# Sparse attention into a mixture of experts on one core: both groups of sparse scores in one stretch, the block list as one row

## The chip, the cores and the metric

The kernel runs on one core of a Trainium2 chip. The metric is the device time of one execution in microseconds (us). The engines are named as in the profile: PE is TensorE (its weight loads are listed apart, as PEld), DVE is VectorE, ACT is ScalarE, POOL is GpSimd, SP is SyncE, which here only issues DMAs. TensorE writes to PSUM, which has eight banks.

## The reference, cut to what matters

Attention over 4 batches x 8 heads x 768 positions x 64, in blocks of 32 (24 blocks). A block of queries sees its own block and the two neighbours, the first and the last block, and three sampled blocks; the first and last query blocks see everything. The result goes, token by token, through a top-1 mixture of eight experts.

```python
mask = np.abs(blk_i - blk_j) <= window                      # window = 1
mask = mask | (blk_i == 0) | (blk_j == 0) | (blk_i == n_blocks - 1) | (blk_j == n_blocks - 1)
for qb in range(n_blocks):
    for kb in sampled_blocks[qb]:                           # three of 24, drawn at random
        mask[qb * block:(qb + 1) * block, kb * block:(kb + 1) * block] = True
scores = np.where(mask, scores, -1000000000.0)              # scores = q @ k.T / 8
attn = softmax(scores); x = (attn @ v) as (3072 tokens, 512)
logits = x @ w_gate + modality_bias[modality_id]
e_idx = argmax(logits); gate_w = softmax(logits)[e_idx]
out = gate_w * (relu(x @ w1[e_idx]) @ w2[e_idx])            # 512 -> 1024 -> 512, 8 experts
```

## The kernel before, in words

**Work items.** Attention is cut into items. A dense item ("d", batch, pair of heads) computes the two query blocks that see everything; there are 16, eight for each half of the batches. A sparse item ("s", half, m, n, b) belongs to a pair m of inner query blocks (11 pairs), query block n of the pair and batch b of the half. Scores of one (half, m, n) are computed for both batches and all heads at once, into two PSUM banks, so a pair m has two groups of scores, n=0 and n=1. The text of the prediction calls one (half, m) a sparse item; there are 22, numbered 0 to 21.

**Stages.** Each item passes stages named by letters: S scores (`dense_scores` L372, `scores` L525, TensorE), M mask and minimum or maximum (`masked` L537 with the operation at L541, VectorE), X exp (`exps` L546, ScalarE), T transposes (L558, L411, TensorE), A copy of the transposes out of PSUM (L563, L418), W weighing of the values (L580, L433), V the row sums and the sampled blocks' values (L573, L589), O division (L440 to L442), Y and G transpose and gate (L596, L606). The banks of scores are free when M of both batches has read them.

**Order.** The kernel writes the order of every engine's program out by hand (`tc.manual_schedule`). The start follows the list START of tokens: an upper case token such as `S00` is a stage of an item, `tb` is one step of the generator `tables()`, `SP16` sixteen such steps, `kl` a load of queries, `qp` the gathering of keys (`share_k` L462), `vl`, `vs` and `v` the gathering of values, `h` a tick's other work, `blk` the reading of the block list (L212). After that a loop over ticks runs stages in the order `OXTSMGVAYW`; in tick t each stage handles the item t minus that stage's lag (S 0, M 1, X 2, T 4, A 4, W 5, V 7, O 8, Y 10, G 13). A sparse pair takes four ticks; scores for n=0 come in the first of them and for n=1 in the third. PSUM banks come from a pool of eight; a matmul into a bank waits until its last readers are done.

**Gathered keys.** `share_k` on GpSimd copies the key blocks that a pair needs into one of two buffers of twelve slots: slots 0 to 7 for n=0, 4 to 11 for n=1. The sampled blocks are copied by number (L482, twelve copies a pair): the first six go to slots 0 to 2, the last six to slots 9 to 11. GpSimd reads the numbers into registers in `key_numbers` (L457), SyncE in `own_numbers` (L511).

**The start.** SyncE issues, in order: the block list broadcast to 128 partitions (L166, 72 KB), queries and keys of the dense items (`dense_q` L150, `dense_k` L157), values (L163), then the gate's inputs (L178 to L180), then by tokens `kl0` and `kl1` the first sparse queries (L144). TensorE runs 56 warm-up matmuls (L210) of 128x128. GpSimd takes the block numbers out of the list (L213), VectorE turns them to floating point (L243) and builds the mask tables (L247 to L274) and the modality bias (L278 to L288) step by step, sixteen steps before the first dense maximum (L392).

## Time and profile before

| | us |
|---|---|
| median of 3 runs (lowest to highest) | 539.94 (538.39 to 546.9) |
| the profiled execution | 535.39 |
| its span, from first to last instruction | 533.7 |
| PE busy, DVE busy, ACT busy, POOL busy in it | 512.8, 378.7, 335.4, 214.7 |

A row of the timeline gives start, duration, engine, source line, operation, what is written from what, and how many instructions were merged into it; in square brackets the engine's idle time before it and what ended that. "issue" means that it waited for nothing the profile shows. SPq rows are DMA issues, whose durations are the issue and not the transfer. A row of the table of stretches gives the stretch, its length, then busy time and number of instructions of each engine, the granted TensorE clock, the share of the DMA engines' time and GB/s; an instruction that runs over a border is counted in both stretches. In a row of a group (page, part 5) the numbers after the bar are the busy time of the group and the mean ns of one.

### The profile page before, as it was taken

To read this page: it belongs to the slowest core of one execution; us is meant where nothing else is said; L and a number is where in the kernel's file an instruction comes from. 1 tells how busy PE (TensorE), PEld (TensorE's weight loads), DVE (VectorE), ACT (ScalarE), POOL (GpSimd) and SP (SyncE) were. 2 spreads that over 40 slices of the span, in tenths; PEclk is the share of its full clock that TensorE was granted. 3 is DMA by queue.
4 is the path that set the end of the run, shared out by engine and by line. 5 is a ranking of instruction groups with operands and counts; after the bars stand their busy time and mean duration, and the time that the engine had idled before them with its cause. 6 is when DMAs were issued, how large, how long until landed. Compare 5 with 4: busy or idle time off the path is not lost.

```text
span 533.7 us, 19015 instructions
## 1 busy us (share of the span) xinstructions
PE 512.8 (96%) x7298; PEld 433.4 (81%) x7298; DVE 378.7 (71%) x1139; ACT 335.4 (63%) x765; POOL 214.7 (40%) x451
## 2 busy tenths in 40 slices
PE   8999999998999999899999999999999999999995
PEld 6667676776778777788989898998989899898984
DVE  7995588677778999967996655556565555656553
ACT  3689877977888977935456454646545464554552
POOL 3578675666458886123155123030312303031213
PEclk9999999999999999999999999999999999999999
DMA  7985886999646888965788776676757667675740
GB/s 281 339 243 150 234 252 209 249 223 242 205 144 205 209 217 233 277 206 206 237 280 305 237 253 201 239 252 204 239 191 244 211 222 250 206 243 192 249 150 23
DMA packets 49443, 119.44 MB, mean 224 GB/s; under 512 B 7744, under 2 KB 8128, under 8 KB 49344
## 3 DMA queue, kind: packets, MB, share of 16 engines
q1 hardware_dynamic: 45248, 105.02, 64.6%
q0 software_dynamic: 4096, 13.12, 6.9%
q8 instruction: 59, 0.97, 0.8%
q14 instruction: 40, 0.33, 0.2%
HBM read 105.52 MB, written 12.86 MB: 222 GB/s over the span
## 4 chain that ended last, share of the span: by engine, by line
issue 41%; PE 32%; DVE 11%; DMA 7%; POOL 5%; SPq 3%; ACT 1%; POOLq 0%; DVEq 0%; ACTq 0%
PE bank L533 5%; PE bank L558 5%; DMA out<-slot,si 3%; PE bank L589 3%; DVE y L541 3%; POOL slot L736 3%; DMA slot<-v 3%; PE bank L580 2%; POOL out L790 2%; PE bank L606 2%; PE bank L754 1%; PE bank L770 1%; PE bank L771 1%; PE bank L769 1%; PE bank L755 1%
## 5 line engine op out<-in xcount | busy, mean ns | idle before, releaser
L725 DVE TENSOR_TENSOR slot<-slot 128x1024 fp32r<-128x1024 f32 x99 | 122.8, 1245 | 89.5 <-ACT slot L722 87.7
L722 ACT CAST slot<-slot 128x1024 fp32r<-128x1024 f32 x104 | 108.1, 1048 | 104.1 <-PE bank L755 50.1
L754 PE MATMUL bank<-slot 128*128 128x256 f32 x384 | 108.4, 282 | 0.0
L756 PE MATMUL bank<-slot 128*128 128x256 f32 x384 | 107.7, 281 | 0.0
L755 PE MATMUL bank<-slot 128*128 128x256 f32 x384 | 107.6, 280 | 0.0
L790 POOL DMA_INDIRECT out<-slot,si x20 | 25.4, 1270 | 178.6 <-ACT slot L786 175.6
L549 ACT ACTIVATE a<-y,mn 128x256 f32<-128x256 f32 x176 | 88.6, 511 | 10.3 <-DVE mn L541 10.2
L769 PE MATMUL bank<-slot 128*128 128x512 f32 x192 | 76.6, 399 | 0.0
L770 PE MATMUL bank<-slot 128*128 128x512 f32 x192 | 75.9, 395 | 0.0
L771 PE MATMUL bank<-slot 128*128 128x512 f32 x192 | 75.7, 394 | 0.0
L754 PEld LDWEIGHTS bank<-slot 128*128 128x128 f32 x384 | 72.2, 188 | 0.6
L755 PEld LDWEIGHTS bank<-slot 128*128 128x128 f32 x384 | 72.1, 188 | 0.4
L756 PEld LDWEIGHTS bank<-slot 128*128 128x128 f32 x384 | 72.2, 188 | 0.0
L541 DVE CUSTOM_DVE_ANT_1 y<-bank,smask 128x256 f32<-128x256 f32 x176 | 66.3, 417 | 0.4
L482 POOL COPY slot<-slot 128x128 f32 x264 | 63.9, 295 | 0.0
L563 ACT COPY at<-bank 128x512 f32<-128x512 f32 x88 | 50.7, 577 | 9.9 <-PE bank L558 9.9
L504 POOL TENSOR_SCALAR slot<-slot 32x1024 f32<-32x1024 f32 x40 | 41.6, 1041 | 35.4 <-issue 11.6
L558 PE MATMUL bank<-ident,a 128*128 128x128 f32 x352 | 51.9, 280 | 0.8 <-ACT a L401 0.5
L533 PE MATMUL bank<-slot,q_raw 64*32 64x256 f32 x1408 | 49.4, 382 | 1.5 <-issue 0.6
L771 PEld LDWEIGHTS bank<-slot 128*128 128x128 f32 x192 | 36.1, 188 | 8.4
L770 PEld LDWEIGHTS bank<-slot 128*128 128x128 f32 x192 | 36.1, 188 | 7.8 <-DVE slot L725 0.4
L558 PEld LDWEIGHTS bank<-ident,a 128*128 128x128 f32 x352 | 38.1, 140 | 4.9 <-ACT a L549 0.8
(302 smaller groups left out, 852.9 us busy)
## 6 DMA issues: line engine op xcount, KB each, us to landing
slot<-w SPq DMA_DIRECT2D x100, 512.0 KB, 4.1
slot<-v SPq DMA_DIRECT2D x180, 128.0 KB, 3.9
x_d<-xr SPq DMA_DIRECT2D x22, 256.5 KB, 5.0
q_raw<-qH SPq DMA_DIRECT2D x22, 256.0 KB, 4.8
slot<-v SPq DMA_DIRECT2D x16, 256.0 KB, 4.6
slot<-kD SPq DMA_DIRECT2D x13, 256.0 KB, 4.3
slot<-v SPq DMA_DIRECT2D x4, 768.0 KB, 11.8
slot<-w SPq DMA_DIRECT2D x10, 256.0 KB, 4.1
```

The costliest lines, as they stand in the source:

```text
L533: nc.tensor.matmul(sp[u][32 * pr:32 * pr + 32, b * 256:(b + 1) * 256], lhsT=q[r, b * NPAIR + pr, n, :], rhs=kv[r, s0:s0 + 8, b, pr, :], st ...
L541: nc.vector.tensor_tensor_reduce(y[:, u, :].rearrange("p (s f) -> p s f", s=8), sp[u][:, b * 256:(b + 1) * 256].rearrange("p (s f) -> p s ...
L549: nc.scalar.activation(a[:, u, :], y[:, u, :], AF.Exp, bias=mn[:, u:u + 1], scale=-1.0, accum_out=total[:, u:u + 1])
L558: nc.tensor.transpose(tp[:, k:k + P], a[:, u, c * P:(c + 1) * P], ident)
L722: nc.scalar.copy(h, s)
L725: (eng or (nc.gpsimd if n in POOL_SPLITS else nc.vector)).tensor_tensor(l, s, h.bitcast(F32), ALU.subtract)
L754: nc.tensor.matmul(o, lhsT=h[:, fs], rhs=xh[g % 2][:, c, :], start=c == 0 and f % 2 == 0, stop=False)
L755: nc.tensor.matmul(o, lhsT=h[:, fs], rhs=xl[g % 2][:, c, :], start=False, stop=False)
L756: nc.tensor.matmul(o, lhsT=l[:, fs], rhs=xh[g % 2][:, c, :], start=False, stop=c == 3 and f % 2 == 1)
L769: nc.tensor.matmul(o, lhsT=hh[0][:, f, ts_], rhs=h[:, fs], start=f == 0, stop=False)
L770: nc.tensor.matmul(o, lhsT=hh[0][:, f, ts_], rhs=l[:, fs], start=False, stop=False)
L771: nc.tensor.matmul(o, lhsT=hl[f // 4][:, f % 4, ts_], rhs=h[:, fs], start=False, stop=f == 7)
```

## The change

1. For every sparse pair but the very first, TensorE computes the scores of n=0 and n=1 directly after one another, at the place of n=0. M and all later stages stay where they were.
2. The block list is loaded as one row (1 partition, 576 bytes) on ScalarE's DMA queue. The numbers, cast to bf16 by VectorE, are spread to 128 partitions by a matmul with a row of ones, between the warm-up matmuls, which are now 14 before and 24 after it; VectorE copies the result out of PSUM.
3. The mask tables are built by GpSimd: ten steps where sixteen of VectorE's stood (the cast of the numbers is no step of the tables any more), and eleven between the two batches' key copies of the first pair. Five `tb` tokens remain, for the modality bias on VectorE.
4. SyncE issues the first piece of keys first, then queries, then the other keys. The gate's inputs are issued by a new token `sm` after `kl1`. GpSimd reads the first pair's key numbers right after the list.

```diff
-WARM = 56
+WARM = (14, 24)
 START = """
-blk SP16 S00 S01 M00 S02 M01 X00 T00 X01 M02 T01 M03 X02 A00 T02 X03 A01 T03 kl0 S10 S11 A02 tb tb M10 A03 tb tb X10 M11 qp0
-W00 X11 O00 W01 tb tb T10 O01 A10 W02 kl1 T11 S12 S13 O02 A11 M12 W03 X12 M13 S0000 S0001 h8 X13 O03 T12 M0000 A12 M0001 W10
+blk SP10 S00 S01 M00 S02 M01 X00 T00 X01 M02 T01 M03 X02 A00 T02 X03 A01 T03 kl0 S10 S11 A02 M10 A03 X10 M11 qp0
+W00 X11 O00 W01 T10 O01 A10 W02 kl1 sm T11 S12 S13 O02 A11 M12 W03 X12 M13 S0000 S0001 h8 X13 O03 T12 M0000 A12 M0001 W10
...
-        blk_raw = const.tile([P, NB * 3 * 2], I32, name="blk_raw")
-        nc.sync.dma_start(blk_raw, blocks.bitcast(I32).rearrange("a b -> (a b)").partition_broadcast(P))
-        dense_q(0, 0, 4)
+        blk_raw = const.tile([1, NB * 3 * 2], I32, name="blk_raw")
+        nc.scalar.dma_start(blk_raw, blocks.bitcast(I32).rearrange("a b -> (a b)").unsqueeze(0))
...
-        dense_k(0)
+        dense_k(0, (0,), ((0, 16),))
+        dense_q(0, 0, 4)
+        dense_k(0, (0,), ((16, 24),))
+        dense_k(0, (1,))
         dense_q(0, 4, 8)
         dense_k(1, (0,))
         dense_v(0)
         dense_k(1, (1,))
         dense_v(1)
-        nc.sync.dma_start(wg_raw, ...)
-        nc.sync.dma_start(mod_raw..., ...)
-        nc.sync.dma_start(b_raw..., ...)
+
+        def gate_inputs():
+            nc.sync.dma_start(wg_raw, ...)
+            nc.sync.dma_start(mod_raw..., ...)
+            nc.sync.dma_start(b_raw..., ...)
...
         warm = bank()
-        for _ in range(WARM):
-            nc.tensor.matmul(warm[:, 0:P], lhsT=onesb, rhs=onesb, start=True, stop=True)
+        ids = blk_raw.rearrange("p (n t) -> p n t", t=2)[:, :, 0:1].rearrange("p n t -> p (n t)")
+        spread_ids = bank()
+
+        def warm_up(n):
+            for _ in range(n):
+                nc.tensor.matmul(warm[:, 0:P], lhsT=onesb, rhs=onesb, start=True, stop=True)

         def block_ids():
-            nc.gpsimd.tensor_copy(rb_i, blk_raw...)
+            nc.gpsimd.tensor_copy(rb_i, ids)
+            key_numbers(0)
...
             nc.vector.tensor_copy(iota_f, iota_i)
+            nc.vector.tensor_copy(rb_b, ids)
+            warm_up(WARM[0])
+            nc.tensor.matmul(spread_ids[:, 0:NB * 3], lhsT=onesb[0:1, :], rhs=rb_b, start=True, stop=True)
+            warm_up(WARM[1])
+            nc.vector.tensor_copy(rb, spread_ids[:, 0:NB * 3].rearrange("p (n t) -> p n t", t=3))
             nc.vector.tensor_scalar(desc, iota_f[:, 0:E], -1.0, float(E), ALU.mult, ALU.add)
...
         def tables():
-            nc.vector.tensor_copy(rb, rb_i.rearrange("p (n t) -> p n t", t=3))
-            yield
-            nc.vector.tensor_tensor(t0, rb, iota_f[:, 0:NB].unsqueeze(2).broadcast_to([P, NB, 3]), ALU.subtract)
+            nc.gpsimd.tensor_tensor(t0, rb, iota_f[:, 0:NB].unsqueeze(2).broadcast_to([P, NB, 3]), ALU.subtract)
             yield
...
@@ share_k
             for bs in ((0,), (1,)) if g == 0 else (range(HB),):
+                if bs == (1,):
+                    spare(11)
                 if m < 2:
...
-        loads = {"blk": block_ids}
+        loads = {"blk": block_ids, "sm": gate_inputs}
...
                 if op == "S":
                     if b == 0:
-                        sp = scores(qraw[m, half], half * NM + m, n)
-                        for b_ in range(HB):
-                            st["s", half, m, n, b_] = sp
+                        for n_ in (n,) if (half, m) == (0, 0) else range(2) if n == 0 else ():
+                            sp = scores(qraw[m, half], half * NM + m, n_)
+                            for b_ in range(HB):
+                                st["s", half, m, n_, b_] = sp
```

All 21 operations of the mask tables (seven on 128x72 elements, twelve on 128x24, two on 128x33) go from `nc.vector` to `nc.gpsimd` in the same way as the one shown.

More of the change, by code (lines that the diff above doesn't have):

```diff
@@ L155, in dense_k @@
             for c in cs:
-                for j0, j1 in js or (((0, 16), (16, 24)) if (b, c) == (0, 0) else ((0, 24),)):
+                for j0, j1 in js or ((0, 24),):
                     nc.sync.dma_start(kd[b][:, c, j0:j1, :].rearrange("p j f -> p (j f)"), kD[b, :, c, j0 * 64:j1 * 64])
@@ L177, in attention_moe @@
         dense_v(1)
-        nc.sync.dma_start(wg_raw, w_gate.rearrange("(c p) e -> p c e", p=P))
-        nc.sync.dma_start(mod_raw.rearrange("p n t -> p (n t)"), modality.bitcast(I32))
-        nc.sync.dma_start(b_raw.rearrange("p a e -> p (a e)"), bias.rearrange("a e -> (a e)").partition_broadcast(P))
+        def gate_inputs():
+            nc.sync.dma_start(wg_raw, w_gate.rearrange("(c p) e -> p c e", p=P))
+            nc.sync.dma_start(mod_raw.rearrange("p n t -> p (n t)"), modality.bitcast(I32))
+            nc.sync.dma_start(b_raw.rearrange("p a e -> p (a e)"), bias.rearrange("a e -> (a e)").partition_broadcast(P))
         onesb = const.tile([P, P], BF16, name="onesb")
@@ L196, in attention_moe @@
         code = const.tile([P, NT], F32, name="code")
-        rb_i = const.tile([P, NB * 3], I32, name="rb_i")
+        rb_i = const.tile([1, NB * 3], I32, name="rb_i")
+        rb_b = const.tile([1, NB * 3], BF16, name="rb_b")
         rb = const.tile([P, NB, 3], F32, name="rb")
```

25 lines of the change are left out of this document (12 added, 13 removed).

## The prediction

> **What bounds the kernel now.** I read the page's busy times first, then the table of stretches, then TensorE's own timeline in one item of the sparse phase, then the first 24 us.
>
> ```profile
> PE 512.8 (96%) x7298; PEld 433.4 (81%) x7298; DVE 378.7 (71%) x1139; ACT 335.4 (63%) x765; POOL 214.7 (40%) x451
> ```
> ```profile
> core 0: us, PE busy (x) PEld busy (x) DVE busy (x) ACT busy (x) POOL busy (x), PEclk, DMA share, GB/s
> 10.00:20.00 10.00, 8.99 (x139) 6.40 (x132) 9.12 (x34) 8.27 (x29) 2.86 (x12) 1.00 1.04 382
> ...
> 30.00:40.00 10.00, 9.04 (x201) 6.80 (x186) 9.64 (x44) 8.14 (x28) 9.27 (x31) 1.00 0.84 242
> 100.00:120.00 20.00, 19.16 (x494) 14.83 (x502) 14.20 (x75) 16.25 (x53) 12.55 (x37) 1.00 0.92 224
> 200.00:220.00 20.00, 17.91 (x445) 13.60 (x441) 19.18 (x95) 17.28 (x52) 9.12 (x18) 1.00 0.90 245
> 300.00:400.00 100.00, 100.00 (x646) 90.45 (x645) 60.78 (x66) 52.08 (x64) 19.89 (x18) 1.00 0.68 224
> ```
>
> Three regimes. Up to 40 us VectorE is nearly full (9.1 to 9.6 us of 10) and TensorE follows it. In the body of the sparse phase TensorE is the fullest (19.16 of 20) and VectorE has room (14.20). Around 200 to 220 us VectorE is full again (19.18). From then on the experts keep TensorE at 100.00 of 100, so that whatever is saved before simply moves the end. The diff touches the first two regimes; no operation of the experts changes.
>
> **Scores in one stretch.** For 21 of the 22 sparse items the second group of scores (query block n=1) moves from two ticks later to right behind the first. No matmul is added or removed, so what can be saved is the cost of entering and leaving the stretch. TensorE's weight loads, and the matmuls of one stretch cut into windows:
>
> ```profile
> 149.97 0.20 PEld L431 LDWEIGHTS bank<-su,ident 128*64 128x64 f32 x4 [0.17 <-issue]
> 150.94 0.42 PEld L558 LDWEIGHTS bank<-ident,a 128*128 128x128 f32 x4
> 151.52 0.61 PEld L533 LDWEIGHTS bank<-slot,q_raw 64*32 64x32 f32 x32 [0.17 <-issue]
> 152.55 0.20 PEld L431 LDWEIGHTS bank<-su,ident 128*64 128x64 f32 x4 [0.41 <-DVE rd L447]
> ```
> ```profile
> 151.50:151.70 0.20, 0.17 (x8) 0.18 (x16) 1.00 0.37 144
> 151.70:151.92 0.22, 0.22 (x16) 0.16 (x9) 1.00 0.13 19
> 151.92:152.13 0.21, 0.21 (x24) 0.15 (x8) 1.00 0.00 0
> ```
>
> A stretch holds TensorE from 151.52 to 152.55, 1.03 us. It enters 0.17 after the transposes and the next work follows 0.41 after its last weight load. But the 0.41 is not all lost time: each window of 0.21 to 0.22 us brings eight more matmuls (the counts, 8, 16, 24, include those still running), so the 32 go in four rounds of about 0.215, and the 0.41 falls into the last round's running out. A second stretch appended to the first therefore costs four more rounds, 4 x 0.215 = 0.86, where it costs 1.03 alone. The entry of 0.17 is not saved either: what then follows the transposes at the old place is the 64- or 32-column work, and L431 at 149.97 enters after transposes with the same 0.17. That is 0.17 per item, 21 x 0.17 = 3.5 us off TensorE. Some two items lie in 200 to 220 us, where VectorE is full and the saving need not arrive: 3.2.
>
> The Trainium skill, TensorEngine Tiling (Array Packing), Key Properties, says that a change of the tiling mode drains TensorE. By that rule alone one would book entry and exit, 0.17 + 0.41 = 0.58 for each item, 12.2 us in all; it is rival A.
>
> **The banks that this takes.** The second group's two PSUM banks are now taken about 0.86 us after the first group's start, and held till VectorE reads them (L541) on ticks 3 and 4. TensorE then waits wherever fewer than two of the eight banks are free. An ordinary place, and the two tight ones:
>
> ```profile
> 103.56 1.09 PE L533 MATMUL bank<-slot,q_raw 64*32 64x256 f32 x32
> 104.08 0.42 DVE L541 CUSTOM_DVE_ANT_1 y<-bank,smask 128x256 f32<-128x256 f32 x1
> 104.13 0.62 ACT L563 COPY at<-bank 128x512 f32<-128x512 f32 x1
> ```
> ```profile
> 138.00 1.18 PE L533 MATMUL bank<-slot,q_raw 64*32 64x256 f32 x32
> 139.57 0.47 ACT L402 ACTIVATE a<-bank,nb__3730 128x256 f32<-128x256 f32 x1
> ```
> ```profile
> 209.03 1.09 PE L533 MATMUL bank<-slot,q_raw 64*32 64x256 f32 x32
> 210.25 0.15 DVE L440 TENSOR_SCALAR rt<-bank 128x8 f32<-128x8 f32 x1
> ```
>
> At 103.56 + 0.86 = 104.42 five banks are taken: two of the new scores, two of the item before (their last readers, L541, run 104.08 to about 104.8), one of a transpose (its copy L563 ends at 104.75). Three are free, no wait. At 138.86 seven are taken, four of them by dense scores, and the second free bank comes with the exp (L401) that ends where L402 begins, 139.57: 0.7. At 209.89 all eight are taken and two free themselves by 210.40: 0.5. Everything TensorE places between the two old spots (gate, weighing, transposes) runs with two banks fewer but also 0.86 later, which by the same count covers all but another 0.7 in the item at 209. Sum 1.9 as a ceiling on this trace; TensorE already waits in part there, so I take 1.0. A gain is excluded, since the banks are only held longer; the upper bound is in rival B. The second group also needs GpSimd's last six key copies sooner by the two ticks:
>
> ```profile
> 101.60 2.89 POOL L482 COPY slot<-slot 128x128 f32 x12
> 107.50 1.09 PE L533 MATMUL bank<-slot,q_raw 64*32 64x256 f32 x32
> ```
>
> These twelve belong to item 10 (counted from 0) and end at 104.49, 3 us before even the second scores of item 9 begin. I cost that at nothing; were the lead gone, TensorE would wait for the last six, up to half of 2.89.
>
> **The start.** Rows of the first 24 us:
>
> ```profile
> 0.80 0.40 SPq L166 DMA_DIRECT2D blk_raw<-blocks  x1
> 0.80 1.28 ACT L215 ACT_TABLE_LOAD   x1 [0.80 <-PEq L1439]
> 1.13 5.54 PE L210 MATMUL bank<-onesb 128*128 128x128 bf16 x56 [1.13 <-DVE onesb L207]
> 1.73 1.37 SPq L157 DMA_DIRECT2D slot<-kD  x3
> 4.21 0.24 POOL L213 COPY rb_i<-blk_raw 128x72 int32<-128x72 int32 x1 [2.21 <-DMA blk_raw<-blocks]
> 6.60 1.52 PE L379 MATMUL bank<-slot,qd 64*64 64x512 f32 x16
> 8.18 0.68 DVE L392 TENSOR_REDUCE nm<-bank 128x1 f32<-128x512 f32 x1
> 8.92 1.15 POOL L470 TENSOR_SCALAR slot<-slot 128x256 f32<-128x256 f32 x3 [4.47 <-DMA slot<-kD]
> 14.74 1.52 PE L379 MATMUL bank<-slot,qd 64*64 64x512 f32 x16
> 15.87 0.69 DVE L392 TENSOR_REDUCE nm<-bank 128x1 f32<-128x512 f32 x1 [0.42 <-PE bank L379]
> 17.12 0.18 DVE L267 TENSOR_SCALAR t<-t 128x24 f32<-128x24 f32 x1
> 18.62 1.14 POOL L470 TENSOR_SCALAR slot<-slot 128x256 f32<-128x256 f32 x3 [7.14 <-issue]
> 19.61 0.18 DVE L272 TENSOR_SCALAR smask<-rm 128x33 f32<-128x33 f32 x1
> ```
> ```profile
> 3.00:5.00 2.00, 2.00 (x22) 2.00 (x20) 1.00 0.79 249
> 5.90:6.50 0.60, 0.60 (x13) 0.59 (x11) 1.00 1.06 420
> ```
>
> The list goes from SyncE to ScalarE's queue, where it can be issued at 0.80 as before. It landed about 3.4 us after issue (GpSimd starts on it at 4.21). It is now one row instead of 128, which may land sooner; no row shows by how much. A new chain hangs on it: VectorE's cast (some 0.2, like GpSimd's 0.24), TensorE's spreading matmul, 24 warm-ups. While TensorE waits for the cast, the warm-ups and the first scores are queued behind it; behind VectorE's two waits are ten small constants, for which it has until the first reduction. The warm-ups run at 0.10 us each before 5.9 us (20 loads in 2.00) and at 0.055 after (11 in 0.60). So: 4.2 + 0.2 + 0.1 + 24 x 0.10 = 6.9 for the first scores, against 6.60. The keys are issued 0.93 earlier (0.80 for 1.73), so with a much faster landing of the list the scores could start at 5.7; these are the ends.
>
> VectorE's first reduction starts 1.13 after such a stretch does (14.74 to 15.87), at 8.0 in place of 8.18, where it stood behind the mask tables. Of the six table operations after 15 us the first two fall into its idle 0.42, the other four last about 0.18 each (rows at 17.12 and 19.61) and partly overlap: 0.6 gained on a VectorE that is full up to 40 us. So 0.8 at TensorE's full pace; with the early end 1.3 + 0.6 = 1.9, with a slow pace (rival C) a loss of 0.4. I take 0.3, between the two paces.
>
> Hidden, in my sum at nothing: 21 table operations on GpSimd, at the 0.24 of L213 to the 0.38 apiece of L470 are 2.4 to 3.8 us before the key copies at 8.92 and 2.6 to 4.2 between the two groups of copies, in idle stretches of 4.47 and 7.14; uncovered they would push the copies by what exceeds these. ScalarE's issue stands before a table load that nothing waits for until the first exp. GpSimd's register loads of the first key numbers move ahead to the landing of the list, into the same idle time. On SyncE's queue the three gate loads go behind the first two query loads and their register reads:
>
> ```profile
> 11.62 4.54 SPq L179 DMA_DIRECT2D mod_raw<-modality  x1
> 17.02 4.28 SPq L144 DMA_DIRECT2D q_raw<-qH  x3
> ```
>
> SyncE stood 4.54 at the modality load and came to the queries at 17.02; now the queries pass, and the value loads of the first items stay behind the gate loads as they were. The sooner queries buy nothing where VectorE is full. If the modality list came late, VectorE would stand at its cast with masked scores behind it.
>
> **Sum.** 3.2 - 1.0 + 0.3 = 2.5 us. The profiled execution took 535.39 with a span of 533.7, so 532.9 with a span of 531.2. The runs' median is 539.94, 4.55 above that execution; on that scale I forecast 537.4.
>
> **Rivals.** *A, each switch costs its drain.* Joining saves entry and exit, 0.58 x 21 = 12.2, and with the start 12.5: 527.4. For it: both gaps are there at every stretch. Against it: the rounds at 0.215 and the entry of 0.17 at L431. Chance 0.07.
>
> *B, banks.* The second group waits in every item for one evacuation, and TensorE, which was ahead, now runs at the heels of VectorE and ScalarE.
> At one copy of 0.62 (L563 at 104.13) per item that is 21 x 0.62 = 13.0 us against the 3.5 saved: 9.5 slower, 549.4. It decides from the point where fewer than two banks are free at the first group's end in most items, or 0.17 us of new wait per item. Against it: three free banks at 104.42, and two or more, counted in the same way, in 19 of 21 items. Waits in half of the items would give 6.5 - 3.5 = 3.0, or 542.9. Chance of a result above the time before by this: 0.16.
>
> *C, the clock.* The pause in the warm-up (from 1.13 + 14 x 0.10 = 2.5 to about 4.5) keeps TensorE at the slow pace, which before ended by 5.9, after 4.8 us without a pause. The first scores then take twice as long, VectorE begins at 6.9 + 2.26 = 9.2, and the start loses 0.4 instead of gaining 0.3: 538.1 with the stretches, or about 540 if these save nothing either (no visible change, chance 0.15). The Trainium skill, TensorE: Matmul & The Clock Gate, Part 1, says that about 3.4 us of sustained work lift the clock; the 0.10 and 0.055 agree in kind, and a pause that restarts the count would make C the rule. Whether it does, no row here shows.
>
> **Chances.** Forecast (0.5 to 6 us saved) 0.62, A 0.07, B 0.16, C with nothing saved 0.15. Range: the forecast's best case, 3.5 + 1.9 = 5.4 with no bank wait, gives 534.5, and the fastest run lies 1.5 below the median (538.39): 533. Saving a part of the drains too would reach 532. Upwards C at 540 and B in nearly half of the items, 542.5. Two per cent, 10.8 us, is about what a measurement of this kernel tells from no change: faster by that is A, 0.07; slower is B beyond its own price, 0.04; the rest, 0.89, lies within.
>
> **What would show it.** Joined stretches should have 64 weight loads, span about 1.89 us from first load to the next work, and no wait over 0.1 inside except at the two tight items; 2.05 would refute the rounds, and following work sooner than 0.3 would favour A. Waits of L533 on ACT or DVE in many items are B. The pace of the last 24 warm-ups and of the first L379 stretch (its first reduction after 1.13 or after twice that) decides C. VectorE's first reduction should come near 8.0. A gain above 6 us would mean that something outside my terms, such as the queue order of the loads, was on the path.

## The result, and the profile after

The changed kernel took 542.7 us (median of 6 runs, 540.69 to 544.32), the kernel before 537.25 us beside it (6 runs, 530.47 to 546.9): a ratio of 1.0131, 95% interval 1.0093 to 1.0169. It is slower by 1.3%, some 7 us. All ratios leave out runs more than 1.5% above the fastest of their kernel, here two of the six before; by the medians of all runs the loss is 5.5 us, and four later ratios, measured beside twelve such runs of 23 (seven banks, later weighing, joined for items 1 to 4 and for items 5 to 21), are 0.005 to 0.009 lower. 537.4 was forecast from a median of 539.94, a gain of 2.5 us or a ratio of 0.995; measured was a loss. The profiled execution took 542.72, its span was 541.0, against 535.39 and 533.7 before.

The page's busy times after, and the table of stretches, with the stretches of the prediction and two more (stretch, length, then busy us and instructions of TensorE, its weight loads, VectorE, ScalarE and GpSimd, the granted clock, DMA share, GB/s):

```profile
PE 514.9 (95%) x7281; PEld 439.0 (81%) x7281; DVE 369.0 (68%) x1119; ACT 335.6 (62%) x765; POOL 223.2 (41%) x472
```
```profile
10.00:20.00 10.00, 9.34 (x146) 6.83 (x139) 8.61 (x28) 7.02 (x23) 7.61 (x29) 1.00 1.03 397
30.00:40.00 10.00, 9.99 (x277) 8.19 (x254) 8.50 (x41) 8.81 (x31) 9.76 (x33) 1.00 0.74 223
100.00:120.00 20.00, 17.83 (x507) 14.62 (x515) 14.27 (x78) 15.34 (x49) 12.58 (x36) 1.00 0.88 213
120.00:140.00 20.00, 17.05 (x365) 13.01 (x357) 12.16 (x51) 14.04 (x45) 10.82 (x35) 0.91 0.84 230
200.00:220.00 20.00, 18.16 (x455) 13.98 (x451) 16.39 (x89) 15.49 (x47) 10.12 (x21) 1.00 0.81 229
220.00:240.00 20.00, 18.00 (x412) 15.86 (x411) 17.22 (x86) 13.99 (x36) 5.00 (x5) 0.91 0.80 205
300.00:400.00 100.00, 100.00 (x643) 90.15 (x642) 60.55 (x66) 52.30 (x65) 18.68 (x16) 1.00 0.69 229
```

Up to 40 us it went as hoped and better: TensorE is busy for 9.99 of 10 us where it was for 9.04, and VectorE is no longer the fullest (8.50 for 9.64). In the body TensorE is less busy: 17.83 of 20 us between 100 and 120 us, before 19.16. It did not become idle because others were full: VectorE has 14.27 as before, ScalarE less. The experts are unchanged at 100.00, so what was lost moved the end.

Where it was lost can be read from the same events in both traces. The scores of item 4 come 2.9 us sooner than before (48.31 for 51.19), those of item 12 1.5 later (139.46 for 138.00), those of item 21 5.1 later (214.10 for 209.03), and the first matmul of the experts 7.1 later (237.7 for 230.6). So some 3 us are gained by 50 us and some 10 lost between 60 and 235 us. Not all of the 10 belongs to the change: in this execution TensorE's clock was half for 3.4 us at 124 and again at 227 (last section), which costs up to 3.4 us together, and the profiled execution before had no such stretch. Over the runs this nearly evens out: the mean granted clock is 0.993 in the six runs after and 0.994 in the 34 runs of the kernel before that stand beside the second measurement of the start alone, a difference worth 0.8 us.

The second group itself mostly does not wait: in 13 of the 21 joined stretches the last weight load follows the first by 1.37 to 1.45 us, where a single group takes 0.505; that is the 0.86 of the prediction. Most of the waiting is behind it, at other work. TensorE's waits (weight loads; the line, what it waited for, us in all, times, longest us) from 28 to 240 us, first before, then after:

```profile
PEld bank L580 <- issue: 3.7, 6, 2.0
...
PEld bank L573 <- ACT at L563: 1.8, 3, 1.0
PEld bank L580 <- ACT at L563: 1.7, 2, 1.0
```
```profile
PEld bank L587 <- ACT at L577: 3.2, 10, 0.8
...
PEld bank L594 <- ACT at L577: 1.9, 2, 1.5
PEld bank L594 <- POOL slot L518: 1.7, 2, 0.9
...
PEld bank L547 <- DVE xr L454: 0.8, 1, 0.8
...
PEld bank L547 <- ACT a L413: 0.7, 1, 0.7
```

These rows have to be read with care. A row counts the whole gap, the ordinary one at that change of work included (0.17 us behind transposes, 0.41 behind scores), and the work it names is the last to have ended before the start, not always the one that was awaited. What was awaited follows from the kernel's program: which bank each matmul writes to, and who reads that bank last before it.

The first row is an example. L587 (L573 before) is stage V's first matmul, the row sums. Ten of its gaps end behind L577, ScalarE's copy of transposes out of PSUM, before three. V doesn't read that copy: the transposes are those of the next item. Where it really waits, it waits for their bank. But five of the ten gaps are the ordinary ones; what is beyond them is 1.1 us in the ten, and 0.6 in the three before. Likewise the row that names GpSimd (L518): GpSimd had ended some 9 us earlier, and both times the weighing waited for a bank that a dense item's exp (L413) read until 0.16 us before. One of V's real waits, at item 13, in both kernels (start, duration, engine, line), before:

```profile
166.09 0.47 PEld L558 LDWEIGHTS bank<-ident,a 128*128 128x128 f32 x4
166.72 0.61 PEld L533 LDWEIGHTS bank<-slot,q_raw 64*32 64x32 f32 x32 [0.17 <-issue]
167.75 0.16 PEld L573 LDWEIGHTS bank<-rexp,fold 128*32 128x32 f32 x8 [0.41 <-ACT xT L598]
```
```profile
166.47 0.56 ACT L563 COPY at<-bank 128x512 f32<-128x512 f32 x1
```

and after:

```profile
169.79 0.47 PEld L572 LDWEIGHTS bank<-ident,a 128*128 128x128 f32 x4
170.77 0.16 PEld L587 LDWEIGHTS bank<-rexp,fold 128*32 128x32 f32 x8 [0.51 <-ACT at L577]
```
```profile
170.16 0.56 ACT L577 COPY at<-bank 128x512 f32<-128x512 f32 x1
```

Before, the second group (L533, 166.72 to 167.75) stands between the transposes and V. The copy ends at 167.03, under it, and V goes on with the usual exit gap. After, the group is gone from this place, V follows the transposes directly, the copy ends at 170.72 and V starts at 170.77.

How full the banks are can be counted from the trace: a bank is taken from the first weight load that writes to it to the end of the last instruction that reads it. The last column of the table has TensorE's waits for a bank: the gaps before weight loads that start within 0.13 us of the end of their bank's last reader (within 0.27 where that is an exp, whose sums are read out after it), each without the ordinary gap of that change of work. All from 28 to 240 us, each from one execution:

| kernel | banks taken, mean | second group's banks held, us | TensorE's waits for a bank, us |
|---|---|---|---|
| before | 5.27 | 5.5 | 5.3 |
| after | 6.19 | 9.9 | 12.1 |

(With the banks that the program assigns, the means are 5.4 and 6.2.) Of the 12.1 us the scores wait for 3.1 (before 0.1), the weighing for 2.6 (1.2), the sparse transposes for 2.4 (1.1), V for 1.4 (1.0) and the dense transposes for 1.1 (0.7). No wait of this kind lies between 28 and 62 us, before the first dense scores among the sparse items. The second group itself waits for a bank in five of the 21 joined stretches.

### The profile page after: what moved, and what is told of

It reads as the page before. It is cut to its first block, busy times and chain, and to the rows that moved or that the text cites. A ratio compares the mean times of both kernels' runs of the same rounds, so it can differ in the third digit from the quotient of the medians.

```text
span 541.0 us, 18972 instructions
## 1 busy us (share of the span) xinstructions
PE 514.9 (95%) x7281; PEld 439.0 (81%) x7281; DVE 369.0 (68%) x1119; ACT 335.6 (62%) x765; POOL 223.2 (41%) x472
## 4 chain that ended last, share of the span: by engine, by line
issue 41%; PE 29%; DMA 11%; POOL 7%; DVE 5%; ACT 2%; SPq 1%; POOLq 1%; ACTq 0%
PE bank L547 6%; PE bank L572 5%; PE bank L594 3%; PE bank L603 3%; POOL slot L750 3%; DMA x_d<-xr 3%; DMA slot<-v 3%; DMA out<-slot,si 2%; PE bank L445 2%; POOL out L804 2%; PE bank L620 2%; PE bank L391 2%; DMA slot<-x_d,gi 2%; PE bank L610 1%; PE bank L423 1%
## 5 line engine op out<-in xcount | busy, mean ns | idle before, releaser
L563 ACT ACTIVATE a<-y,mn 128x256 f32<-128x256 f32 x176 | 88.5, 509 | 7.6 <-DVE mn L555 7.2
L518 POOL TENSOR_SCALAR slot<-slot 32x1024 f32<-32x1024 f32 x40 | 42.7, 1067 | 56.3 <-PE bank L603 23.4
L577 ACT COPY at<-bank 128x512 f32<-128x512 f32 x88 | 50.6, 577 | 17.0 <-PE bank L572 17.0
L572 PE MATMUL bank<-ident,a 128*128 128x128 f32 x352 | 54.0, 286 | 2.0 <-issue 0.7
L547 PE MATMUL bank<-slot,q_raw 64*32 64x256 f32 x1408 | 46.8, 380 | 3.4 <-issue 2.1
```

What stands on the lines that cost most here:

```text
L547: nc.tensor.matmul(sp[u][32 * pr:32 * pr + 32, b * 256:(b + 1) * 256], lhsT=q[r, b * NPAIR + pr, n, :], rhs=kv[r, s0:s0 + 8, b, pr, :], st ...
L563: nc.scalar.activation(a[:, u, :], y[:, u, :], AF.Exp, bias=mn[:, u:u + 1], scale=-1.0, accum_out=total[:, u:u + 1])
L572: nc.tensor.transpose(tp[:, k:k + P], a[:, u, c * P:(c + 1) * P], ident)
```

## The experiments

Ratios are to the kernel before, measured beside each, with 95% intervals; a thousandth is 0.54 us. Differences of two ratios have the two intervals' half widths added in squares. The table at the end has the bank counts and the waits for banks.

### Which part of the change costs

The start alone: in the changed kernel both groups are back at their places.

```diff
-                        for n_ in (n,) if (half, m) == (0, 0) else range(2) if n == 0 else ():
+                        for n_ in (n,):
```

> The changed kernel, with the second group of scores back at its old place; all changes of the start stay. Banks theory (the second group holds two PSUM banks two ticks longer, TensorE waits for them): the gain of the start stays, first sparse scores about 0.7 and the fourth item's about 2.7 sooner than in the kernel before, and nothing is lost between 60 and 235 us: 0.5 to 3.5 us faster than before, ratio 0.993 to 0.999. Start theory (what is lost in the middle comes from the sooner start, which brings GpSimd's copies, loads and TensorE's code fetches into other positions): slower than before by some 5 us, ratio 1.005 to 1.015, as with the whole change.

0.9979 (0.9945 to 1.0012), 535.18 us. The same kernel on another chip:

> The kernel with the start's changes alone once more, on the chip of the three others of this call, so that they can be compared with it: by the first measurement 0.9979 of the kernel before, 0.9945 to 1.0012. The traces' marks say 0.4 to 0.9 us sooner first scores: 0.998 to 0.999.

0.9988 (0.9955 to 1.0022), 536.84 us. Both lie together at 0.9984 (plus or minus 0.0024): the start alone gains perhaps 0.9 us and loses nothing, so the start theory falls.

The joined scores alone, in the kernel before (the same line added there):

> The kernel before, with only the two groups of scores joined. Banks theory: 4 to 10 us slower than before, ratio 1.008 to 1.018, with the first sparse scores where they were (23.5 us in the trace) and waits of TensorE for bank readers above those of before by 6 to 10 us between 60 and 240 us. Start theory: 2 to 4 us faster, the 0.16 us that each joined stretch saves.

1.0144 (1.0101 to 1.0188), 544.27 us. All of the loss belongs to the joined scores. V's row of the changed kernel is there as well (without the ordinary gaps 2.0 us, of 12.9 us of waits for banks):

```profile
PEld bank L573 <- ACT at L563: 3.8, 10, 0.8
```

### Is it the banks

One PSUM bank fewer in the kernel before, until the experts begin:

```diff
-        psum = actx.enter_context(tc.tile_pool(name="psum", bufs=8, space=PSUM))
+        psum = actx.enter_context(tc.tile_pool(name="psum", bufs=7, space=PSUM))
+        psum8 = actx.enter_context(tc.tile_pool(name="psum8", bufs=1, space=PSUM))
...
-        hp, op, xp = [bank() for _ in range(4)], [bank() for _ in range(2)], [bank() for _ in range(2)]
+        hp, op, xp = [psum8.tile([P, 512], F32, name="bank8")] + [bank() for _ in range(3)], [bank() for _ in range(2)], [bank() for _ in range(2)]
```

> The kernel before, with seven PSUM banks instead of eight for everything until the experts begin; nothing else is changed. In the traces the attention holds 5.27 banks on average before and 6.19 after the change, 0.92 more. Banks theory: one bank fewer costs about what the change costs, without its savings: 7 to 14 us slower than before, ratio 1.013 to 1.026. If banks are not short (order, code fetches or the clock make the loss): ratio 0.997 to 1.004.

1.0107 (1.0065 to 1.0148), 541.31 us. Below the range of the banks theory, but well above what "not short" allowed, 1.004: the kernel before already lives at the edge of its banks. By the medians of all runs the ratio is 1.0053, so the price of a bank lies somewhere between 3 and 6 us. In its trace TensorE waits 14.6 us for banks, the scores above all, and most often for the transposes' copy:

```profile
PEld bank L534 <- ACT at L564: 4.7, 6, 1.3
```

Next, the banks held without joining. In the changed kernel only the first 2 of the second group's 16 calls stay at the early place, which are 4 of its 32 matmuls in the trace (`scores` is given which of its matmuls to do, and the banks):

```diff
-                        for n_ in (n,) if (half, m) == (0, 0) else range(2) if n == 0 else ():
+                        for n_ in (n,) if (half, m) == (0, 0) else range(2) if n == 0 else (1,):
...
+                            elif n == 0:
+                                sp = scores(qraw[m, half], half * NM + m, n_, slice(0, 2) if n_ else slice(0, 32))
+                            else:
+                                sp = scores(qraw[m, half], half * NM + m, 1, slice(2, 32), st["s", half, m, 1, 0])
```

> The changed kernel, but only 2 of the second group's 32 matmuls stay directly behind the first group; the other 30 are back at the old place. The two banks are thus taken as early as in the changed kernel and held as long, while the work between the places is delayed by no more than one round of 0.2 us. Banks theory: as slow as the changed kernel or up to 4 us slower (the saved entries and exits are lost again): ratio 1.010 to 1.022, and at least 3 us slower than the kernel with the start's changes alone. Order theory: as fast as the kernel with the start's changes alone, give or take 2 us.

1.0129 (1.0089 to 1.0169), 543.5 us: as slow as the changed kernel. But the expectation left out that the early matmuls, added to 21 items, are on TensorE's path, and they take more than one round: a stretch with them lasts 1.42 us in the trace where one group takes 1.02, and the other 28 at the old place still take 1.01. So the control, with the same additional matmuls into banks that are taken anyway:

```diff
+                            if n == 0 and (half, m) != (0, 0):
+                                scores(qraw[m, half], half * NM + m, 0, slice(0, 2), sp)
```

> The kernel with the start's changes alone; behind the first group of each item but the first, TensorE does its first two matmuls once more, into the same banks. So TensorE has the same additional early round (0.22 us, 21 times: at most 4.5 us) as the kernel that held the second group's banks with two early matmuls, but no bank is taken sooner. Banks theory: 1 to 4.5 us slower than the start's changes alone (535.2 there), 536 to 540 us, and at least 3 us faster than the held banks (543.5). If the delay of the work between the two places were the cause, not the banks: 542 to 545 us.

1.0075 (1.0043 to 1.0107), 541.14 us. Against the start alone that is 0.0091, 4.9 us. Its stretches, too, last 1.42 us, so that TensorE has 21 x 0.40 = 8.4 us more to do, not the 4.5 of the expectation; some six tenths of it reach the end. Holding the banks costs 0.0054 (plus or minus 0.0051), 2.9 us; not nothing, but not the 8 us that the changed kernel loses against the start alone. In the two traces the waits for banks differ by more, 10.8 us to 4.8. The delay theory gets no support: 0.40 us of delay for each item cost less than the time that TensorE spends on it. The 0.86 of the changed kernel wasn't tested apart from the banks.

### What holding does not explain: the lost cover

The second group behind the stage that followed it (V, or the gate G), in the kernel with the start alone. No bank is held longer; the cover of the copy is gone:

```diff
+                            if op == "S" and kind == "s" and items[k][3] == 1:
+                                continue
...
+                    if op == "V" and t < NI and items[t][0] == "s" and items[t][3] == 1:
+                        do("S", items[t])
```

> The kernel with the start's changes alone; the second group of each item moves a little later, behind the gate or the row sums and sampled values (stages G and V) that stood directly behind it. No bank is taken sooner or held longer. Cover theory (the second group's own stretch of 1.03 us stood between the transposes and V or G, and covered the copy that empties the transposes' bank, which V then takes; in the changed kernel V waits 10 times, 3.2 us, for that copy, before 3 times, 1.8 us): V waits as in the changed kernel, 3 to 8 us slower than the start's changes alone (0.998): ratio 1.004 to 1.013. Hold theory (only the longer holding of the second group's banks costs): 0.995 to 1.000.

0.9997 (0.9968 to 1.0026), 536.76 us: 0.7 us above the start alone, within the uncertainty. The cover theory by itself falls. V waits once:

```profile
PEld bank L587 <- ACT at L577: 0.2, 1, 0.2
```

With banks to spare V simply has another one. Then both together: the kernel with held banks, and these same lines in it, so that the second group's other 28 matmuls stand behind V:

> The kernel with held banks (two early matmuls of the second group, ratio 1.0129), with the other 30 matmuls behind the stages G and V instead of ahead of them. Taking the cover away alone cost nothing (0.9997 against 0.998 to 0.999). Theory of both together (V waits for the transposes' copy only where the held banks leave it no other bank, and only where no stretch stands between): 3 to 9 us slower than with the held banks alone, ratio 1.018 to 1.030. If the two do not act together: 1.012 to 1.016.

1.0219 (1.0162 to 1.0276), 548.2 us (the median of six, one of which took 2789.91 and isn't in the ratio): 0.0090 (plus or minus 0.0070), 4.8 us, above the held banks, where taking the cover away alone cost 0.7. That points to the two acting together, but the difference of the two prices, 4.1 us, has an uncertainty of 4.3, so the times alone don't show it. The traces say the same: V waits 4.4 us for banks, 1.1 with held banks alone, and all of TensorE 14.4 where it was 10.8; taking the cover away alone brought 3.7, the start alone 3.2 and 3.5. V's row, first with held banks and then with the cover gone as well:

```profile
PEld bank L589 <- ACT at L579: 1.7, 3, 0.8
```
```profile
PEld bank L589 <- ACT at L579: 3.9, 9, 0.9
```

Against the control with the additional matmuls it is 0.0144 (plus or minus 0.0065), 7.7 us for both without any joining. The joined scores cost 0.0147 (plus or minus 0.0045) more than the start alone, 7.9 us, and save 0.16 for each of 21 items, so 11.3 before their saving if that arrived in full. The missing 3.6 us are within the uncertainty of the two numbers and are not resolved. In the changed kernel itself V has the smaller part: it waits 1.4 us of the 12.1 for banks.

### Where joining costs

Joined for items 1 to 4 alone, and for items 5 to 21 alone (the second line in place of the first):

```diff
+                        for n_ in (n,) if (half, m) == (0, 0) or half * NM + m > 4 else range(2) if n == 0 else ():
...
+                        for n_ in (n,) if half * NM + m < 5 else range(2) if n == 0 else ():
```

> The changed kernel with joined scores for items 1 to 4 only, which lie before the first dense scores among the sparse items (61 us in the changed kernel's trace); later items have the second group at its old place. Banks theory (joining costs only where TensorE then finds no free bank): the four items keep their gain, which by the marks of the two traces is 2.9 us at item 4's scores against 0.9 us for the start alone, and nothing is lost later: 532.5 to 534.5 us where the kernel with the start's changes alone took 535.2, ratio to before 0.992 to 0.997. Equal-cost theory (each joined stretch loses about the same, 7.5 us over 21 stretches): 1.4 us slower than the start's changes alone, ratio 1.000 to 1.001.

> The changed kernel with joined scores for items 5 to 21 only; items 1 to 4 have the second group at its old place. Banks theory: all of the loss lies here, and the gain of items 1 to 4 is missing: 1 to 3 us slower than the changed kernel, 543.5 to 546 us, ratio 1.013 to 1.019. Equal-cost theory: 17 of 21 stretches, 17/21 of 7.5 us on top of 535.2, 541.2 us, ratio 1.009.

1.0036 (0.9981 to 1.0091), 535.67 us, and 1.0165 (1.0091 to 1.0239), 543.61 us. The two were measured together, and their medians lie 7.9 us apart, where the equal-cost theory has 4.6 for 17 stretches against 4. The loss lies mainly from item 5 on, where dense items come in between, as the banks theory has it and as the traces show it: 4.1 us of waits for banks in the first kernel, 14.2 in the second. (The 1.009 of the equal-cost theory is just outside the interval of 1.0165; by the medians of all runs that kernel is at 1.0095, so this number alone doesn't exclude it.) The gain of the first four, which the marks had promised, did not reach the end: the median is that of the start alone.

### Giving banks back

The second group masked one tick sooner:

```diff
+                            if op == "M" and kind == "s" and items[k][1:3] != (0, 0) and items[k][3:] in ((0, 1), (1, 0)):
+                                do(op, (*items[k][:3], 1, 0 if items[k][3] == 0 else 1))
```

> The changed kernel with VectorE's masking of the second group one tick sooner, so that its banks come free one tick sooner; exps and transposes stay where they were. Banks theory: half or more of the 9 us of new bank waits goes, 3 to 8 us faster than the changed kernel, ratio to the kernel before 0.997 to 1.007. Order theory (the work between the two old places, transposes and weighing, comes 0.86 later and its consumers wait, whatever the banks do): no change to the changed kernel, or slower since VectorE's copies now stand behind more masking: ratio 1.010 to 1.02.

1.0098 (1.0061 to 1.0136), 541.57 us: not the 3 us that were expected, at best 1.8. The edit did not do what it was for: the second group's banks are held for 9.2 us instead of 9.9, not a tick less, since VectorE does its masking in the order of its queue and the first group's banks are held as long as before. V's row stays at 3.3 us in 10 waits, and TensorE's waits for banks are the most of all kernels, 16.8 us, though the time is not: these waits are not simply added to the time. The weighing one tick later:

```diff
-'s': {'S': 0, 'M': 1, 'X': 2, 'T': 4, 'A': 4, 'W': 5, 'V': 7, 'O': 8, 'Y': 10, 'G': 13}
+'s': {'S': 0, 'M': 1, 'X': 2, 'T': 4, 'A': 4, 'W': 6, 'V': 7, 'O': 8, 'Y': 10, 'G': 13}
```

> The changed kernel with the weighing of the shared values (the stage W of the sparse items) one tick later, so that its bank, held 6.1 us in the trace of the changed kernel, is held for about one tick (1.9 us) less; all other stages stay. Over 22 items this gives back some 40 of the 185 bank-microseconds that joining takes (42 banks held 4.4 us longer). Banks theory: 1 to 3 us faster than the changed kernel, ratio to before 1.008 to 1.012. Order theory (delays of TensorE's work, not banks): no gain, or slower since the weighing now stands directly before the sampled values: ratio 1.013 to 1.020.

1.015 (1.0072 to 1.0227), 542.62 us: no gain can be seen. The weighing's bank was held for 4.9 us instead of 6.1, so 27 bank-microseconds came back, not 40. V's row went from 10 waits to 3, but the time did not follow; TensorE waited elsewhere, 13.9 us for banks in all. That reads as if a bank given back here were taken by the next one who lacked it.

Both groups at the second place, where the cover stays and the first group's banks are taken later; masking and exps of the first group move a tick later (the loop over ticks that uses `later` is left out here, and so is the list START, from which item 1 loses its first place):

```diff
+        def both_at(half, m):
+            return (half, m) != (0, 0) and at["s", half, m, 1, 0] == at["s", half, m, 0, 0] + 2
+        def later(op, it):
+            return int(it[0] == "s" and op in "MX" and it[3] == 0 and both_at(*it[1:3]))
...
-                        for n_ in (n,) if (half, m) == (0, 0) else range(2) if n == 0 else ():
+                        for n_ in range(2) if n == 1 and both_at(half, m) else () if both_at(half, m) else (n,):
```

> The kernel with the start's changes; both groups of scores run in one stretch, but at the second group's old place, two ticks later than in the changed kernel; masking and exp of the first group move one tick later with it (items 0, 5, 7 and 11 stay unjoined). The stretch stays between the transposes and V, and the first group's banks are held for a shorter time. Banks and cover theory: the 0.16 us per joined item arrives and no wait of V is added: 1 to 4 us faster than the start's changes alone, ratio 0.990 to 0.997, and 9 to 12 us faster than the changed kernel. If joining itself costs (any order in which 1.9 us of scores run at once makes VectorE and ScalarE wait and then TensorE): ratio 1.005 to 1.015.

1.0045 (1.0012 to 1.0078), 538.58 us: more than half of the loss is gone, and so is the shortage (3.8 us of waits for banks, 5.31 banks taken), but the expected gain isn't there. The transposes now come too soon after the exps that they read (L563), a wait for data; V's seven gaps are mostly the ordinary 0.41 behind scores (1.2 us beyond it):

```profile
PEld bank L572 <- ACT a L563: 5.5, 10, 1.7
PEld bank L587 <- ACT at L577: 3.8, 7, 1.1
```

The exps half a tick sooner on ScalarE's queue, at the end of the tick in which they are masked:

```diff
+                k = t - LAG["s"]["X"]
+                if 0 <= k < NI and later("M", items[k]):
+                    do("X", items[k])
                 hook(7)
```

> The kernel joined at the second place, with the first group's exps at the end of the tick in which they are masked, about half a tick sooner on ScalarE's queue. In the trace of the kernel joined at the second place, few groups of TensorE start on a bank just released, but its transposes waited 10 times, 5.5 us in all, for the exps of the same items, which had moved a tick later. If those waits are what was left of the loss: ratio 0.993 to 1.000 in place of 1.0045. If joining costs for another reason: 1.003 to 1.010.

1.0111 (1.0052 to 1.017), 540.63 us, slower still. A good part of that may be the clock: its mean is 0.988 in these six runs and 0.994 in the ten of the kernel before this one, which is worth some 3 us. The waits for exps stayed, and the copies, now behind the exps, came later for V (2.0 us beyond the ordinary gaps):

```profile
PEld bank L587 <- ACT at L577: 5.5, 9, 1.3
PEld bank L572 <- ACT a L563: 5.4, 10, 1.7
```

So no joined order that was measured comes below the kernel before. One with V ahead of the transposes wasn't measured. The kernel with the start alone is the best of all, and at 0.9984 it can't be told from the kernel before.

### The start in parts

The mask tables back on VectorE (in all 21 steps of `tables`), and the list as before; both in the kernel with the start alone:

```diff
-            nc.gpsimd.tensor_tensor(t0, rb, iota_f[:, 0:NB].unsqueeze(2).broadcast_to([P, NB, 3]), ALU.subtract)
+            nc.vector.tensor_tensor(t0, rb, iota_f[:, 0:NB].unsqueeze(2).broadcast_to([P, NB, 3]), ALU.subtract)
...
```
```diff
-        nc.scalar.dma_start(blk_raw, blocks.bitcast(I32).rearrange("a b -> (a b)").unsqueeze(0))
+        nc.sync.dma_start(blk_raw, blocks.bitcast(I32).rearrange("a b -> (a b)").partition_broadcast(P))
...
+            nc.gpsimd.tensor_copy(rb, rb_i.rearrange("p (n t) -> p n t", t=3))
...
+            warm_up(56)
```

> The kernel with the start's changes alone, with the 21 steps of the mask tables on VectorE instead of GpSimd. VectorE theory (the start gains because the tables leave a VectorE that is busy all the time up to 25 us): the gain goes, first sparse scores at 23.4 us or later where they were at 22.8 to 23.2 with the tables on GpSimd and at 23.5 before. List theory (it gains because the list lands sooner and lets the dense scores start at 5.2 to 5.6 in place of 6.6): the gain stays, 22.8 to 23.2.

> The kernel with the start's changes alone, with the block list broadcast to 128 partitions on SyncE's queue and one run of 56 warm-ups, as before; tables stay on GpSimd. VectorE theory: first sparse scores still at 22.8 to 23.2 us. List theory: 23.4 or later, first dense scores at 6 to 6.6 us.

1.0009 (0.9972 to 1.0047) and 0.9982 (0.9947 to 1.0017): at the end neither can be told from the start alone. In the traces the first sparse scores come at 23.3 with the tables on VectorE, at 24.1 with the list as before, at 23.2 and 22.6 with both changes (two executions), 23.5 before. With the list as before, the dense scores stand behind 56 warm-ups:

```profile
1.12 5.99 PE L217 MATMUL bank<-onesb 128*128 128x128 bf16 x56 [1.12 <-DVE onesb L211]
7.20 1.52 PE L386 MATMUL bank<-slot,qd 64*64 64x512 f32 x16
```

Their start at 7.2 is 0.6 above what was expected, and the first sparse scores at 24.1 speak for the list theory; the tables' part (23.3) is too small against the 0.6 by which two executions of one kernel differ.

| kernel | ratio | banks taken, mean | second group's banks held, us | TensorE's waits for a bank, us |
|---|---|---|---|---|
| start alone, first and second measurement | 0.9979, 0.9988 | 5.09, 5.06 | 5.4, 5.3 | 3.2, 3.5 |
| cover removed | 0.9997 | 4.93 | 4.1 | 3.7 |
| joined for items 1 to 4 | 1.0036 | 5.25 | 5.9 | 4.1 |
| joined at the second place | 1.0045 | 5.31 | 5.8 | 3.8 |
| sooner mask | 1.0098 | 6.23 | 9.2 | 16.8 |
| seven banks | 1.0107 | 5.20 of 7 | 5.6 | 14.6 |
| held banks | 1.0129 | 6.07 | 10.1 | 10.8 |
| joined only | 1.0144 | 6.20 | 10.2 | 12.9 |
| later weighing | 1.0150 | 6.15 | 10.0 | 13.9 |
| joined for items 5 to 21 | 1.0165 | 6.12 | 9.6 | 14.2 |
| held banks, cover removed | 1.0219 | 6.08 | 9.9 | 14.4 |

The two sides part clearly: up to 1.0045 TensorE waits 3 to 4 us for banks, from 1.0098 on 11 to 17. Within the second half the waits of one execution don't order the times.

## Why the prediction was wrong

**The rounds were right.** A joined stretch has its last weight load 1.37 us after the first, and the next work comes with the same exit gap, so that the second group costs 0.865 where it cost 1.02 alone: 0.16 an item, as the sum had it; from the first load to the next work it is 1.89 us, as forecast. Whether those 3.4 us reach the end in full is not shown: the first four joined items brought nothing that can be seen. Rival A falls with it: nothing of the drains was saved beyond that. The Trainium skill, TensorEngine Tiling (Array Packing), Key Properties, has the drain at a change of mode; the trace shows a gap at both ends of a joined stretch as of a single one, and one pair of gaps less is worth 0.16 us here.

**The banks failed: the term of 1.0 us, with its ceiling of 1.9.** The counting at the first group's end was right. With the banks that the program assigns, five, seven and eight are taken at the three places, and two or more are free in 19 of 21 items; at the two tight ones the second group then waited 0.7 and 1.1 us, where 0.7 and 0.5 stood. What failed is the step behind it, the sentence that the work between the old places "runs with two banks fewer but also 0.86 later, which by the same count covers all but another 0.7". It counted the banks at the instant in which the second group takes them, and not over the two ticks for which it then holds them. With some 0.9 banks more taken on average, TensorE waits 12.1 us for banks, where the start alone has 3.2 and 3.5: 9 us more, of which the scores have some 3 and everyone behind them the rest. The seven-bank kernel says the same without any joining: a bank fewer costs 1.07%, 5.7 us (2.8 by the medians), so "three are free" at one instant said little.

A second step may have failed with it. What the prediction removed at the old place it treated as cost only; but the second group's 1.03 us were also the cover under which ScalarE emptied the transposes' bank before V took it. What is late next, once that stretch is gone, was not asked. Holding costs 2.9 us, and the lost cover on top of it 4.8, where alone it costs 0.7; all three have large uncertainties, and in the changed kernel V's own waits for banks are only 1.4 us. So the banks are shown as the cause by the runs and by the traces; how its price divides between holding and cover stays open. A ceiling of 1.9 us stood where some 11 were paid.

**Rival B had the right mechanism and the wrong place.** It let the second group wait in every item and gave 9.5 us slower, in half of the items 3.0. It was 7 us, and the second group waited for a bank in five of 21 items; the rest was paid by the weighing, the transposes and V. Its point of decision, fewer than two free banks at the first group's end in most items, was not reached, so by its own test it would have been dismissed; that 7 lies between its two numbers is luck.

**The start was better than its term.** The list's row was on ScalarE's queue at 0.80 and VectorE began on it at 2.05 without a wait; the prediction had kept the 3.4 us that the broadcast took.

```profile
0.80 0.52 ACTq L166 DMA_DIRECT2D blk_raw<-blocks  x1
...
2.05 0.19 DVE L236 CAST rb_b<-blk_raw 1x72 bf16<-1x72 int32 x1
...
2.73 0.24 PE L238 MATMUL bank<-rb_b,onesb 1*128 1x72 bf16 x1
2.90 2.22 PEld L219 LDWEIGHTS <-onesb 128*128 128x128 bf16 x24
...
5.22 1.52 PE L391 MATMUL bank<-slot,qd 64*64 64x512 f32 x16
...
6.34 0.69 DVE L404 TENSOR_REDUCE nm<-bank 128x1 f32<-128x512 f32 x1 [1.28 <-PE bank L391]
...
9.16 0.66 PE L391 MATMUL bank<-slot,qd 64*64 64x512 f32 x4 [2.42 <-DMA slot<-kD]
```

So the first scores came at 5.22 instead of 6.9, and the reduction at 6.34 instead of 8.0. The second scores then waited 2.42 us for keys, and of the 1.8 by which the reduction is sooner than before, 0.7 arrives at the first sparse scores. At the end the start is worth 0.9 us (plus or minus 1.3), where 0.3 was taken, so that the times can't tell the two apart. That the tables on GpSimd cost nothing was right as far as can be seen. So was the lead of GpSimd's key copies, although the profile's answer on the scores' line has three waits for them:

```profile
  POOL slot L496: 1.1, 3
```

Two of the three are the ordinary gap of 0.17, and the third, 0.73 us, is one of the waits without a releaser that the last section describes; what the joined scores really waited for key copies in that trace is 0.2 us.

**Rival C fell.** The pause in the warm-up was 0.2 us, not 2, and the first dense stretch had its reduction 1.12 us after it began, the fast pace.

**The sum as measured:** the stretches -3.4 (21 x 0.16, taken in full), the start -0.9, the banks +11.3, together +7.0, which is what the ratio of 1.0131 says. The 11.3 is not measured by itself but is what the other numbers leave; 7.7 of it were reproduced without joining, and 9 are seen as waits for banks in the trace. The other terms had the right sign, and this one was forecast at less than a tenth of its price.

## What to carry to other kernels

When a stretch of work moves, ask twice what it was good for at its old place: what it cost there, and which copy, load or release ran under it. PSUM banks are a budget over time, not a test at one instant: multiply what is held by how long, add it to the mean that is taken, and find by one kernel with a bank fewer what the marginal bank is worth, before trading banks for 0.16 us a piece. A bank given back at one place seems to go to the next who lacked it: neither repair showed much. And before a row of waits is believed, take off the gap that this change of work has anyway, and check that what it names was awaited.

## What was not expected of the hardware

**Half clock in the middle of the kernel.** After two waits of TensorE its granted clock was half for 3.4 us each. The waits (weight loads), and the stretches after them (the clock is the third number from the end):

```profile
123.12 0.25 PEld L620 LDWEIGHTS bank<-wg_raw,xT 128*64 128x64 f32 x5 [1.94 <-issue]
...
226.03 1.19 PEld L594 LDWEIGHTS bank<-slot,at 128*64 128x64 f32 x29 [1.49 <-ACT at L577]
```
```profile
124.30:127.60 3.30, 3.30 (x21) 2.74 (x21) 1.29 (x7) 1.75 (x5) 3.22 (x12) 0.50 0.96 247
127.70:129.00 1.30, 1.30 (x31) 0.45 (x27) 0.00 (x0) 1.30 (x6) 1.30 (x6) 1.00 0.98 266
226.70:230.00 3.30, 3.30 (x28) 3.18 (x23) 2.82 (x7) 1.88 (x6) 2.90 (x2) 0.50 0.91 275
```

Each cost up to 1.7 us, so a wait of some 1.5 us can cost twice its length. The kernel before had no such stretch in its profiled execution, although one of its waits was 2.0 us; 14 of the 16 traces of the experiments have one to three, the start alone among them. In the 3.41 us before the two slow stretches TensorE was busy for 1.56 and 2.05 us, but in the kernel before there is such a time with 1.77 and no slow stretch after it, so no threshold can be read. In all the traces the time between two changes of the clock is a whole number of 3.41 us (here 119.47, 3.41, 98.99, 3.41), as if it were decided at fixed intervals. The Trainium skill, TensorE: Matmul & The Clock Gate, Part 1, has the half clock after an idle window of about 3.4 us; the length of the slow stretches agrees with that window, but here single waits of 1.94 and 1.49 us, in such a time, were enough.

**Waits without a releaser at fixed places of TensorE's program.** The longest waits put down to "issue" (1.94 us above, 2.0 in the kernel before) come, counted along TensorE's instructions, at positions 193 or 194 after a multiple of 256, and end 1.3 to 1.6 us after a packet of 16 KB on the DMA queue of instructions:

```profile
q8 instruction: 59, 0.97, 0.8%
```

They add up to 7.8 us before and 8.7 after in the profiled executions, so they don't explain the loss; but which of these places wait, and for how long, changes from execution to execution, 1.7 us in the kernel with seven banks and some 10 in that with the start alone, and may be a part of why runs of one kernel lie 10 us apart. That they are fetches of the program is read from the coincidence and wasn't tested.
